# Retention attention and a rational feed-forward: another order of the rounds ahead of the feed-forward

## The chip, the cores and the metric

The kernel runs on one core of one Trainium2 chip. The metric is the device time of one execution in microseconds. Before the change three runs took 1000.58 to 1001.1 us, with a median of 1001.1 us. A separate profiled execution, from which all rows below come, took 999.55 us; the profile's own span, from the first to the last instruction, is 997.8 us of it.

## The reference

Eight batches of 576 tokens with eight heads of 64 go through causal attention with a decay instead of a softmax, and the result, as one matrix of 4608 x 512, through a feed-forward whose activation is a quotient of two polynomials:

```
scores = (1/8) * q @ k.T                       # per batch and head
Dmat[i, j] = gamma[h] ** (i - j) if i >= j else 0
x = ((scores * Dmat) @ v) as 4608 x 512
h = x @ w_in                                   # 512 x 2048
P = a0 + a1*h + a2*h^2 + a3*h^3
Q = 1 + |b0|*|h| + |b1|*h^2
out = (P / (Q + 1e-6)) @ w_out                 # 2048 x 512
```

All data are float32.

## The kernel before

**Attention, in units.** The 4608 tokens are 36 units of 128. For unit n the kernel loads a transposed pair q, k (the tile `qk`) and an untransposed pair k, v (the tile `kv`), 512 KB each (`load_unit`). Then, in this order of need:

- `scale_q(n)` multiplies q by a table of decays: one pass on GpSimd (POOL).
- `scale_v(n)` multiplies v by a decay per head: eight small passes on ScalarE (ACT).
- `scores(n)` forms k times q on TensorE (PE) into a PSUM tile `ps`; `decay(n)` masks it on VectorE (DVE) into `s`.
- `outputs(n)` adds three products on PE into the same `ps`: s with v, k with v (the state's increment, called `ds`), and the running state `S_sb` with q.
- `keep_hi(n)` copies the result to `xhi` on ACT, rounded to the type that the fast matmul takes; `keep_lo(n)` writes what the rounding lost to `xlo` on DVE, and then, on DVE too, adds `ds` to the state `S_sb` (or copies it, for the first unit of a batch).
- `fade(n)` multiplies `S_sb` by a decay on POOL. The next unit's `outputs` needs the faded state.

**Feed-forward, in steps.** There are nine blocks of 512 tokens (four units each) and sixteen slices of the hidden width; a step is one slice of one block. `gemm1` makes a slice h from `xhi` and `xlo`, the `ffn_...` parts compute the activation on ACT, DVE and (for one pass in the first 24 steps) POOL, and `gemm2` adds its product to the block's output, three to four steps later. So that both matmuls are accurate, each of the 32 weight tiles is split once into a rounded and a remaining part: `start` takes the magnitude of the bits on ACT (`c`), `split0` is one pass of DVE on `c`, `split1` and `split2` are one pass each of DVE with the bits as second operand, and `split3` makes the rounded part on ACT (`w`) and the rest on POOL (`w`). The names with a number, such as `c0_3`, `w0_3`, `bits0_3`, mean w_in's tile 3; with 1 in front, w_out's.

**What sets the order.** Each engine executes its instructions in the order in which they are written. A table of names gives this order: `BEFORE` for the rounds ahead of the feed-forward (round n = 0 to 4 handles a new unit n and the outputs of unit n-1), `FIRST` for the first 24 steps, `DENSE` for the next 8, `REST` for all others. `run` walks through the table and calls what is due. `STARTS_BEFORE` and `STARTS` say how many weights are started in each round and each step. Units 4 to 8 are handled inside `FIRST`; units 0 to 3, the first block, must be complete, `xhi` and `xlo`, before the first `gemm1`. All loads are issued by SyncE (SP) in the order in which they are written: units 0 to 5 and eight weights up front, the rest as the steps go; a load also waits until an earlier one has completed, and for its buffer.

Two rules of the framework matter for the change. A PSUM bank of a tile has one reader or writer at a time in the written order, so of two instructions of different engines that read the same `ps`, the second waits for the first. And the score tiles of units 2 and 4 share one PSUM buffer, so `scores(4)` waits until unit 2's `keep_lo` is done.

Of the kernel before, what the change touches and what calls it, by code (L numbers as in the profile page):

```python
# [12 lines left out]
F32 = mybir.dt.float32  # L13
# [17 lines left out]
NP = 4  # L31

BEFORE = "scale_q split1 scale_v split2 split3 start scores outputs decay split0 keep_hi keep_lo fade".split()
FIRST = (
    "split1 gemm1 outputs ffn_p split2 ffn_hi keep_hi ffn_lo gemm2 ffn_r scale_q split3 keep_lo fade start ffn_p2"
    " scale_v scores decay split0 ffn_q ffn_v"
).split()
DENSE = (
    "gemm1 outputs keep_hi split1 keep_lo fade ffn_p split2 split0 ffn_v scale_q ffn_hi ffn_r ffn_lo scale_v gemm2"
    " ffn_p2 scores decay split3 ffn_q"  # L40
).split()
REST = (
    "gemm1 ffn_p outputs keep_hi keep_lo fade ffn_hi ffn_p2 ffn_lo scores decay scale_q scale_v ffn_v gemm2 ffn_r ffn_q"
).split()
END = "ffn_r ffn_hi gemm2 ffn_lo ffn_q".split()

STARTS_BEFORE = [0, 1, 1, 1, 2]
STARTS = [1, 2, 2, 1, 2] + [1] * 19

# [17 lines left out]
def retention_ffn(ctx: ExitStack, tc: tile.TileContext, qkv, w_in, w_out, ab, masks, gq, gv, out):  # L67
# [185 lines left out]
    def keep_lo(n):  # L253

        u = n % 9
        o, ds = parts_of(n)
        hi, lo = (x_part(x, n) for x in x_of(n // 4))
        dve.tensor_tensor(lo, o, hi.bitcast(F32), ALU.subtract)
        if u in (0, 4):
            dve.tensor_copy(S_sb, ds)  # L260
        elif u != 8:
            dve.tensor_tensor(S_sb, S_sb, ds, ALU.add)
        del st_a[n]

# [174 lines left out]
    nc.sync.dma_start(ab_sb, ab)
    for n in range(NP + 1):  # L440
        before(n)
# [10 lines left out]
    for i in range(len(steps) + lag(len(steps))):  # L452
# [63 lines left out]
```

## Time and profile before

| what | us |
|---|---|
| median of three runs | 1001.1 |
| the profiled execution | 999.55 |
| its span | 997.8 |
| first `gemm1` matmul begins | 44.15 |
| PE busy in the span | 934.3 |
| DVE busy in the span | 839.0 |
| ACT busy in the span | 709.0 |
| POOL busy in the span | 158.3 |
| DMA queue for all loads and stores, share of 16 engines | 17.9% |

The rows of the timeline give start, length, engine, operation, the tile written and the tiles read, a count, and in brackets how long the engine was idle before and what ended it. Buffer numbers are left out there, so `ps` stands for each unit's tile. `PEld` is the weight load that goes ahead of a matmul. A line number L63 is that of a helper through which all engine instructions pass, so groups are told apart by tile names. The granted clock of TensorE has a mean of 0.978.

### The profile page before, as it was taken

Reading aid. Unit: us, or ns where it says so; the run is one execution under the profiler, and the core shown is the slowest. Engines: PE = TensorE matmul, PEld = TensorE weight load, DVE = VectorE, ACT = ScalarE, POOL = GpSimd, SP = SyncE. Lnnn points to the kernel's source line nnn. Section 1 sums busy time; section 2 is a strip of 40 time slices with the busy share of each in tenths; the row PEclk is TensorE's granted clock in tenths of the full one; section 3 lists DMA queues with packets and bytes.
Section 4 is the critical chain, followed back from the end, with each engine's and each line's share of the span. In section 5 each row is a group of like instructions: output and inputs, shape, how many; then the busy total and the mean of one; then the engine's idle time right before and its main releaser. Section 6 shows DMA issues by size and latency. Waiting matters only on the chain.

```text
span 997.8 us, 14766 instructions
## 1 busy us (share of the span) xinstructions
PE 934.3 (94%) x5658; PEld 756.3 (76%) x5658; DVE 839.0 (84%) x1189; ACT 709.0 (71%) x1274; POOL 158.3 (16%) x128
## 2 busy tenths in 40 slices
PE   5687878788999999999999999999999999999998
PEld 5566766566787888878888888888878888888886
DVE  3499989999788888888888888988888888888895
ACT  4386777777767777777777777777777777777774
POOL 2444433443100000100000000100000000000000
PEclk8798999999999999999999999999999999999999
DMA  9943100002212111210121112111211121001001
GB/s 359 407 178 127 43 0 1 1 0 82 89 43 85 44 43 43 85 64 22 43 85 43 43 44 85 43 43 43 85 43 43 43 85 44 1 1 43 1 1 42
DMA packets 20550, 65.31 MB, mean 65 GB/s; under 512 B 2304, under 2 KB 2432, under 8 KB 20480
## 3 DMA queue, kind: packets, MB, share of 16 engines
q1 hardware_dynamic: 20480, 64.37, 17.9%
q8 instruction: 44, 0.72, 0.3%
q14 instruction: 26, 0.21, 0.1%
HBM read 54.93 MB, written 9.44 MB: 65 GB/s over the span
## 4 chain that ended last, share of the span: by engine, by line
PE 73%; DVE 16%; ACT 5%; issue 3%; DMA 2%; POOL 0%; SPq 0%; ACTq 0%; POOLq 0%
PE acc L63 33%; PE h L63 31%; PE ps L63 9%; DVE c L63 7%; DVE p L63 6%; DVE v L63 2%; DMA qk<-in_qkv 2%; ACT c L63 1%; ACT u L63 1%; ACT kv L63 1%; ACT o L63 1%; ACT v L63 1%; DMA kv<-in_qkv 1%; ACT g L63 0%; POOL qk L63 0%
## 5 line engine op out<-in xcount | busy, mean ns | idle before, releaser
L63 PE MATMUL acc<-w,g 128*128 128x512 f32 x1632 | 404.9, 397 | 5.2 <-ACT o L63 4.0
L63 PE MATMUL h<-xhi,w 128*128 128x512 f32 x1152 | 381.1, 392 | 17.9 <-DVE p L63 17.2
L63 PEld LDWEIGHTS acc<-w,g 128*128 128x128 f32 x1632 | 305.2, 190 | 77.4 <-ACT o L63 4.8
L63 PEld LDWEIGHTS h<-xhi,w 128*128 128x128 f32 x1152 | 216.5, 188 | 69.4 <-DVE p L63 22.7
L63 PE MATMUL h<-xlo,w 128*128 128x512 f32 x576 | 224.6, 390 | 0.2 <-DVE xlo L63 0.2
L63 ACT ACTIVATE p<-h,ab_sb 128x512 f32<-128x512 f32 x144 | 111.4, 773 | 135.2 <-PE h L63 135.1
L63 DVE TENSOR_TENSOR v<-v,u 128x512 f32<-128x512 f32 x144 | 124.4, 864 | 27.9 <-ACT v L63 27.9
L63 DVE SCALAR_TENSOR_TENSOR p<-p,ab_sb,u 128x512 f32<-128x512 f32 x144 | 108.8, 756 | 27.2 <-ACT u L63 26.4
L63 ACT ACTIVATE u<-h 128x512 f32<-128x512 f32 x144 | 85.7, 595 | 61.8 <-DVE v L63 60.4
L63 DVE TENSOR_TENSOR p<-p,h 128x512 f32<-128x512 f32 x144 | 98.9, 687 | 33.9 <-ACT u L63 33.2
L63 PEld LDWEIGHTS h<-xlo,w 128*128 128x128 f32 x576 | 108.3, 188 | 22.4 <-DVE xlo L63 0.5
L63 ACT ACTIVATE v<-u,absb 128x512 f32<-128x512 f32 x144 | 116.2, 807 | 1.3 <-DVE p L63 1.1
L63 POOL TENSOR_TENSOR S_sb<-S_sb,gv_sb 128x256 f32<-128x256 f32 x32 | 21.8, 680 | 583.3 <-DVE S_sb L63 583.3
L63 DVE SCALAR_TENSOR_TENSOR p<-p,ab_sb,h 128x512 f32<-128x512 f32 x144 | 107.2, 744 | 3.1
L63 ACT ACTIVATE u<-u,lnb 128x512 f32<-128x512 f32 x144 | 104.4, 725 | 4.7
L63 DVE SCALAR_TENSOR_TENSOR p<-v,p 128x512 f32<-128x512 f32 x144 | 101.6, 706 | 5.0
L63 ACT ACTIVATE u<-v,lnb 128x512 f32<-128x512 f32 x144 | 103.1, 716 | 0.1
L63 DVE SCALAR_TENSOR_TENSOR v<-v,u 128x512 f32<-128x512 f32 x144 | 99.4, 690 | 0.0
L63 ACT ACTIVATE g<-p 128x512 fp32r<-128x512 f32 x136 | 85.7, 630 | 8.0 <-DVE p L63 4.3
L63 DVE TENSOR_TENSOR g<-p,g 128x512 fp32r<-128x512 f32 x112 | 77.6, 693 | 1.4 <-ACT g L63 1.4
L63 ACT ACTIVATE kv<-kv,gv_sb 128x64 f32<-128x64 f32 x288 | 72.5, 340 | 6.2 <-DMA gv_sb<-in_gv 5.0
L63 POOL TENSOR_TENSOR qk<-qk,gq_sb 128x512 f32<-128x512 f32 x36 | 59.7, 1660 | 9.5 <-DMA qk<-in_qkv 9.5
(35 smaller groups left out, 634.6 us busy)
## 6 DMA issues: line engine op xcount, KB each, us to landing
qk<-in_qkv SPq DMA_DIRECT2D x36, 512.0 KB, 4.8
kv<-in_qkv SPq DMA_DIRECT2D x36, 512.0 KB, 3.9
bits<-in_w_in SPq DMA_DIRECT2D x16, 512.0 KB, 10.2
bits<-in_w_out SPq DMA_DIRECT2D x16, 512.0 KB, 10.2
out<-o SPq DMA_DIRECT2D x16, 512.0 KB, 3.2
out<-o SPq DMA_DIRECT2D x4, 256.0 KB, 2.3
gq_sb<-in_gq SPq DMA_DIRECT2D x1, 256.0 KB, 2.7
mask_sb<-in_masks SPq DMA_DIRECT2D x1, 128.0 KB, 4.5
```

The lines of the kernel that those rows point to most:

```text
L63: return lambda *a, **k: self.tc.keep_in_program_order(method(*a, **k))
```

## The change

In the rounds ahead of the feed-forward, `scale_q` and `scale_v` are called for unit n+1 instead of unit n, with unit 0 scaled ahead of round 0. In the table they stand at the front of the round, ahead of the fade. The state's addition, until now the second half of `keep_lo`, is a function `add` of its own. In all four tables it stands ahead of `keep_lo`; in `BEFORE` it and the fade stand ahead of `keep_hi` as well. The splits' places in `BEFORE` are others too, and of the weights one is started in round 3 instead of step 1.

```diff
-BEFORE = "scale_q split1 scale_v split2 split3 start scores outputs decay split0 keep_hi keep_lo fade".split()
+BEFORE = "split1 start scale_q scale_v scores decay outputs split2 add fade keep_hi keep_lo split3 split0".split()
 FIRST = (
-    "split1 gemm1 outputs ffn_p split2 ffn_hi keep_hi ffn_lo gemm2 ffn_r scale_q split3 keep_lo fade start ffn_p2"
+    "split1 gemm1 outputs ffn_p split2 ffn_hi keep_hi ffn_lo gemm2 ffn_r scale_q split3 add fade keep_lo start ffn_p2"
     " scale_v scores decay split0 ffn_q ffn_v"
 ).split()
...
-STARTS_BEFORE = [0, 1, 1, 1, 2]
-STARTS = [1, 2, 2, 1, 2] + [1] * 19
+STARTS_BEFORE = [0, 1, 1, 2, 2]
+STARTS = [1, 1, 2, 1, 2] + [1] * 19
...
     def keep_lo(n):
 
+        hi, lo = (x_part(x, n) for x in x_of(n // 4))
+        dve.tensor_tensor(lo, parts_of(n)[0], hi.bitcast(F32), ALU.subtract)
+        del st_a[n]
+
+    def add(n):
+
         u = n % 9
-        o, ds = parts_of(n)
-        hi, lo = (x_part(x, n) for x in x_of(n // 4))
-        dve.tensor_tensor(lo, o, hi.bitcast(F32), ALU.subtract)
+        ds = parts_of(n)[1]
         if u in (0, 4):
             dve.tensor_copy(S_sb, ds)
         elif u != 8:
             dve.tensor_tensor(S_sb, S_sb, ds, ALU.add)
-        del st_a[n]
...
-        todo |= {f.__name__: (f, n) for f in (decay, scale_q, scale_v)}
+        todo["decay"] = decay, n
+        if n < NP:
+            todo |= {f.__name__: (f, n + 1) for f in (scale_q, scale_v)}
         if n >= 1:
-            todo |= {f.__name__: (f, n - 1) for f in (keep_hi, keep_lo, fade)}
+            todo |= {f.__name__: (f, n - 1) for f in (keep_hi, add, keep_lo, fade)}
             todo["outputs"] = (put_out, n - 1)
...
     nc.sync.dma_start(ab_sb, ab)
+    scale_q(0)
+    scale_v(0)
     for n in range(NP + 1):
         before(n)
```

`DENSE` and `REST` change as `FIRST` does (`keep_lo fade` becomes `add fade keep_lo`), and the steps' list of due calls takes `add` in.

**POOL, rounds 2 and 3.** Before, from the fade of unit 1's state on; `qk3` and `qk4` are the queries of units 3 and 4, `w0_1` the remaining part of a weight:

```order
L63 TENSOR_TENSOR S_sb_111<-S_sb_111,gv_sb_93 128x256
L63 TENSOR_TENSOR qk3_131<-qk3_131,gq_sb_94 128x512
L63 TENSOR_TENSOR w0_1_293<-c0_1_240,w0_1_293 128x512
L63 TENSOR_TENSOR S_sb_111<-S_sb_111,gv_sb_93 128x256
L63 TENSOR_TENSOR qk4_139<-qk4_139,gq_sb_94 128x512
```

POOL in the changed kernel, from the queries of unit 3 on; the first fade in it is that of unit 1's state again:

```order
L63 TENSOR_TENSOR qk3_131<-qk3_131,gq_sb_94 128x512
L63 TENSOR_TENSOR S_sb_111<-S_sb_111,gv_sb_93 128x256
L63 TENSOR_TENSOR w0_0_287<-c0_0_188,w0_0_287 128x512
L63 TENSOR_TENSOR qk4_139<-qk4_139,gq_sb_94 128x512
L63 TENSOR_TENSOR S_sb_111<-S_sb_111,gv_sb_93 128x256
```

The queries have moved from behind the fade to in front of it, and the weight's pass stands right behind the fade and belongs to a weight one earlier.

**ACT, rounds 2 to 4.** Before, from `keep_hi(1)` (into `xhi0` from `ps1`) to `keep_hi(3)`:

```order
L63 ACTIVATE xhi0_220<-ps1_190 128x4x128
L63 ACTIVATE kv3_133<-kv3_133,gv_sb_93 128x64 x8
L63 ACTIVATE w0_1_293<-c0_1_240 128x512
L63 ACTIVATE c0_2_296<-bits0_2_135 128x512
L63 ACTIVATE xhi0_220<-ps2_242 128x4x128
L63 ACTIVATE kv4_141<-kv4_141,gv_sb_93 128x64 x8
L63 ACTIVATE w0_2_349<-c0_2_296 128x512
L63 ACTIVATE c0_3_352<-bits0_3_137 128x512
L63 ACTIVATE c1_0_354<-bits1_0_143 128x512
L63 ACTIVATE xhi0_220<-ps3_298 128x4x128
```

ACT in the changed kernel, from the values of unit 3 to the same `keep_hi(3)`:

```order
L63 ACTIVATE kv3_133<-kv3_133,gv_sb_93 128x64 x8
L63 ACTIVATE xhi0_230<-ps1_199 128x4x128
L63 ACTIVATE w0_0_287<-c0_0_188 128x512
L63 ACTIVATE c0_2_292<-bits0_2_135 128x512
L63 ACTIVATE c0_3_294<-bits0_3_137 128x512
L63 ACTIVATE kv4_141<-kv4_141,gv_sb_93 128x64 x8
L63 ACTIVATE xhi0_230<-ps2_247 128x4x128
L63 ACTIVATE w0_1_345<-c0_1_236 128x512
L63 ACTIVATE c1_0_352<-bits1_0_143 128x512
L63 ACTIVATE c0_4_354<-bits0_4_145 128x512
L63 ACTIVATE xhi0_230<-ps3_305 128x4x128
```

Each unit's values now stand ahead of the `keep_hi` of the unit two before it, and the second of the two weights started in round 3 is `c0_3`.

**DVE, rounds 2 and 3.** Before, from `keep_lo(1)` (into `xlo0` from `ps1`) on; `s3` is `decay(3)`:

```order
L63 TENSOR_TENSOR xlo0_221<-ps1_190,xhi0_220 128x4x128
L63 TENSOR_TENSOR S_sb_111<-S_sb_111,ps1_190 128x256
L63 SCALAR_TENSOR_TENSOR c0_1_240<-bits0_1_129,c0_1_240 128x512 x2
L63 TENSOR_TENSOR s3_331<-ps3_298,mask_sb_92 128x1024
L63 TENSOR_SCALAR c0_2_296<-c0_2_296 128x512
L63 TENSOR_TENSOR xlo0_221<-ps2_242,xhi0_220 128x4x128
L63 TENSOR_TENSOR S_sb_111<-S_sb_111,ps2_242 128x256
```

DVE in the changed kernel, from the same `keep_lo(1)` to the two passes of `split0` that follow `keep_lo(2)`:

```order
L63 TENSOR_TENSOR xlo0_231<-ps1_199,xhi0_230 128x4x128
L63 TENSOR_SCALAR c0_1_236<-c0_1_236 128x512
L63 SCALAR_TENSOR_TENSOR c0_1_236<-bits0_1_129,c0_1_236 128x512
L63 TENSOR_TENSOR s3_314<-ps3_305,mask_sb_92 128x1024
L63 SCALAR_TENSOR_TENSOR c0_1_236<-bits0_1_129,c0_1_236 128x512
L63 TENSOR_TENSOR S_sb_111<-S_sb_111,ps2_247 128x256
L63 TENSOR_TENSOR xlo0_231<-ps2_247,xhi0_230 128x4x128
L63 TENSOR_SCALAR c0_2_292<-c0_2_292 128x512
L63 TENSOR_SCALAR c0_3_294<-c0_3_294 128x512
```

The addition to the state has moved ahead of `keep_lo`, and between the two stand three passes on one weight and the mask, where there were the mask and passes on two weights.

**DVE, steps 1 and 2.** Before, from `decay(5)` on; `p`, `v`, `u` are the activation's tiles of steps 0 to 2:

```order
L63 TENSOR_TENSOR s5_520<-ps5_511,mask_sb_92 128x1024
L63 TENSOR_SCALAR c1_1_506<-c1_1_506 128x512
L63 TENSOR_SCALAR c0_5_508<-c0_5_508 128x512
L63 SCALAR_TENSOR_TENSOR p0_0_443<-p0_0_443,ab_sb_95,u0_0_441 128x512
L63 SCALAR_TENSOR_TENSOR v0_0_442<-v0_0_442,u0_0_441 128x512
L63 SCALAR_TENSOR_TENSOR p0_0_443<-v0_0_442,p0_0_443 128x512
L63 TENSOR_TENSOR v0_1_495<-v0_1_495,u0_1_494 128x512
L63 SCALAR_TENSOR_TENSOR c1_1_506<-bits1_1_151,c1_1_506 128x512
L63 SCALAR_TENSOR_TENSOR c0_5_508<-bits0_5_153,c0_5_508 128x512
L63 TENSOR_TENSOR p0_2_578<-p0_2_578,h0_2_535 128x512
L63 SCALAR_TENSOR_TENSOR c1_1_506<-bits1_1_151,c1_1_506 128x512
L63 SCALAR_TENSOR_TENSOR c0_5_508<-bits0_5_153,c0_5_508 128x512
```

DVE in the changed kernel, the same stretch:

```order
L63 TENSOR_TENSOR s5_526<-ps5_517,mask_sb_92 128x1024
L63 TENSOR_SCALAR c0_5_514<-c0_5_514 128x512
L63 SCALAR_TENSOR_TENSOR p0_0_451<-p0_0_451,ab_sb_95,u0_0_449 128x512
L63 SCALAR_TENSOR_TENSOR v0_0_450<-v0_0_450,u0_0_449 128x512
L63 SCALAR_TENSOR_TENSOR p0_0_451<-v0_0_450,p0_0_451 128x512
L63 TENSOR_TENSOR v0_1_503<-v0_1_503,u0_1_502 128x512
L63 SCALAR_TENSOR_TENSOR c0_5_514<-bits0_5_153,c0_5_514 128x512
L63 TENSOR_TENSOR p0_2_582<-p0_2_582,h0_2_539 128x512
L63 SCALAR_TENSOR_TENSOR c0_5_514<-bits0_5_153,c0_5_514 128x512
```

The three passes on one of the two weights are gone from here. They stand in the rounds now.

More of the change, by code (lines that the diff above doesn't have):

```diff
@@ L38 @@
 DENSE = (
-    "gemm1 outputs keep_hi split1 keep_lo fade ffn_p split2 split0 ffn_v scale_q ffn_hi ffn_r ffn_lo scale_v gemm2"
+    "gemm1 outputs keep_hi split1 add fade keep_lo ffn_p split2 split0 ffn_v scale_q ffn_hi ffn_r ffn_lo scale_v gemm2"
     " ffn_p2 scores decay split3 ffn_q"
@@ L42 @@
 REST = (
-    "gemm1 ffn_p outputs keep_hi keep_lo fade ffn_hi ffn_p2 ffn_lo scores decay scale_q scale_v ffn_v gemm2 ffn_r ffn_q"
+    "gemm1 ffn_p outputs keep_hi add fade keep_lo ffn_hi ffn_p2 ffn_lo scores decay scale_q scale_v ffn_v gemm2 ffn_r ffn_q"
 ).split()
 END = "ffn_r ffn_hi gemm2 ffn_lo ffn_q".split()
-STARTS_BEFORE = [0, 1, 1, 1, 2]
-STARTS = [1, 2, 2, 1, 2] + [1] * 19
+STARTS_BEFORE = [0, 1, 1, 2, 2]
+STARTS = [1, 1, 2, 1, 2] + [1] * 19
 SCORES = [1, 3, 5, 23, 25, 27, 29, *range(2 * NF, (NB - 1) * NF, 4)]
@@ L458, in retention_ffn @@
             out_n = due.pop()
-            todo |= {f.__name__: (f, out_n) for f in (keep_hi, keep_lo, fade)}
+            todo |= {f.__name__: (f, out_n) for f in (keep_hi, add, keep_lo, fade)}
             todo["outputs"] = (put_out, out_n)
```

## The prediction

> **What bounds the kernel now.** I read the table of stretches first. Its rows give, for a stretch of the span, its length, the busy time of PE, PEld, DVE, ACT and POOL with their instruction counts, then TensorE's granted clock, the DMA share and GB/s.
>
> ```profile
> 20.00:40.00 20.00, 10.96 (x132) 9.74 (x132) 8.35 (x13) 7.92 (x23) 7.67 (x6) 0.67 1.03 407
> 60.00:80.00 20.00, 13.14 (x96) 10.41 (x94) 19.93 (x26) 14.84 (x29) 10.53 (x8) 0.84 0.08 30
> 112.00:232.00 120.00, 97.08 (x434) 74.50 (x433) 109.48 (x148) 87.84 (x142) 49.39 (x35) 0.98 0.01 1
> 300.00:400.00 100.00, 99.42 (x602) 80.59 (x602) 87.76 (x124) 71.14 (x130) 9.26 (x8) 1.00 0.16 53
> ```
>
> There are three stages. In the rounds no engine is busy for more than 55% (10.96 of 20 us): a loop of waits sets the pace. From the first step to about 232 us DVE does (19.93 of 20, later 109.48 of 120). After that PE does (99.42 of 100). The stages follow each other, and neither of the later two waits for anything that comes by the clock, so what the rounds lose or gain is carried to the end whole. Next, the chain that ended last, in the rounds (start, length, what):
>
> ```profile
> 7.09 9.54 DMA qk<-in_qkv
> ...
> 16.64 9.47 DMA qk<-in_qkv
> ...
> 35.20 0.04 POOL S_sb L63
> 35.24 0.85 issue
> 36.09 1.72 POOL qk L63
> ...
> 37.85 5.62 PE ps L63 x64
> ...
> 43.50 0.61 ACT xhi L63
> ...
> 44.13 0.70 DVE xlo L63
> ```
>
> The loop is fade, scaling of the next queries, scores and outputs, `keep_hi`, `keep_lo`, addition, fade. The timeline of one turn (fade of unit 1 to addition of unit 2):
>
> ```profile
> 24.69 0.41 DVE L63 TENSOR_TENSOR S_sb<-S_sb,ps 128x256 f32<-128x256 f32 x1
> 25.24 0.93 POOL L63 TENSOR_TENSOR S_sb<-S_sb,gv_sb 128x256 f32<-128x256 f32 x1 [5.97 <-DVE S_sb L63]
> 26.13 1.71 POOL L63 TENSOR_TENSOR qk<-qk,gq_sb 128x512 f32<-128x512 f32 x1
> 27.80 1.27 POOL L63 TENSOR_TENSOR w<-c,w 128x512 fp32r<-128x512 f32 x1
> 27.90 2.08 PE L63 MATMUL ps<-qk 64*128 64x128 f32 x16 [4.51 <-POOL qk L63]
> 30.02 1.23 DVE L63 TENSOR_TENSOR s<-ps,mask_sb 128x1024 f32<-128x1024 f32 x1 [3.31 <-PE ps L63]
> 33.41 0.60 ACT L63 ACTIVATE xhi<-ps 128x512 fp32r<-128x512 f32 x1 [5.42 <-PE ps L63]
> 33.90 2.01 ACT L63 ACTIVATE kv<-kv,gv_sb 128x64 f32<-128x64 f32 x8
> 34.04 0.69 DVE L63 TENSOR_TENSOR xlo<-ps,xhi 128x512 fp32r<-128x512 f32 x1 [2.45 <-ACT xhi L63]
> 34.65 0.41 DVE L63 TENSOR_TENSOR S_sb<-S_sb,ps 128x256 f32<-128x256 f32 x1
> ```
>
> One turn is 34.65 - 24.69 = 9.96 us, and POOL, PE, ACT and DVE take it in turn. The queries of unit 3, issued at 7.09, landed at 16.63 but are scaled at 26.13, only because POOL's order puts them behind the fade. (The chain also names a transfer that ends at 26.12, issued at 16.64. That is unit 5's, and I take it for a coincidence; it is a rival below.)
>
> **The change: the rounds.** With the queries and values scaled a round sooner the loop is cut. What is late next is the data. In ACT's new order the values of unit n+1 stand ahead of `keep_hi(n-1)`, so a load holds a `keep_hi`. SP's rows (start and length of the issue), then the loads' times to landing in the same order:
>
> ```profile
> 7.62 0.51 SPq L104 DMA_DIRECT2D kv<-in_qkv  x1
> 12.82 0.33 SPq L104 DMA_DIRECT2D kv<-in_qkv  x1
> 22.93 0.33 SPq L439 DMA_DIRECT2D ab_sb<-in_ab  x1
> ```
>
> ```profile
> kv<-in_qkv SPq DMA_DIRECT2D x1, 512.0 KB, 11.5
> kv<-in_qkv SPq DMA_DIRECT2D x1, 512.0 KB, 11.4
> ab_sb<-in_ab SPq DMA_DIRECT2D x1, 3.0 KB, 9.1
> ```
>
> Unit 3's values land at 19.1, unit 4's at 24.2, the activation's constants at 32.0. SP's order up to there is unchanged, so these times hold. The passes on a weight, in the view of tile `c` (shortest, median, longest, in ns):
>
> ```profile
> L63 DVE SCALAR_TENSOR_TENSOR c<-bits,c x62: 677/686/1785, 15.2 to 226.4; 128x512 int32<-128x512 int32 x62
> L63 ACT ACTIVATE c<-bits x32: 644/652/680, 12.2 to 228.1; 128x512 f32<-128x512 f32 x32
> L63 DVE TENSOR_SCALAR c<-c x32: 415/1068/1514, 12.9 to 229.3; 128x512 int32<-128x512 int32 x32
> ```
>
> Now the new path. Values of unit 3 at 19.1, scaled in 2.01 (21.1); `keep_hi(1)` 0.60 (21.7); `keep_lo(1)` 0.69 (22.4). DVE then has a split pass 0.42, another 0.69, the mask 1.23 and a third pass 0.69: 3.03 (25.4). A POOL pass on a weight lies beside them; for that I add 0.7 (26.1, why see below). Addition 0.41 (26.5), `keep_hi(2)` behind it 0.60 and `keep_lo(2)` 0.69 (27.8). Unit 4's scaled values (24.2 + 2.0 = 26.2) are just in time, so that load is hidden, with 0.3 us to spare. `scores(4)` needs unit 2's buffer and so this `keep_lo`; with `outputs(3)` PE takes 5.5 us, as the piece of 5.62 in the chain shows (33.3). Addition 0.41, `keep_hi(3)` 0.60, and six hand-overs of some 0.03 us: `keep_lo(3)` begins at **34.5 instead of 44.13, 9.6 us sooner**.
>
> The ends of this term. PE is idle for some 5 us before `scores(4)`, and after such an idle time scores take 2.08 us; in the first round they took less:
>
> ```profile
> 6.81 1.16 PE L63 MATMUL ps<-qk 64*128 64x128 f32 x16 [1.98 <-POOL qk L63]
> ```
>
> By that ratio PE would need 3.1 us instead of 5.5, but then DVE is late: two first split passes, two second ones, mask and two third ones are 2 x 0.42 + 4 x 0.64 + 1.23 = 4.6 us. So the term reaches 9.6 + 0.9, and without the 0.7 beside POOL 11.2. Downwards, two full POOL passes (1.27 each) on DVE's line instead of 0.7, and as much behind `scores(4)`, take off some 2.2: 7.4.
>
> **The change: beside POOL.** Two rows of one place in step 2, and DVE's passes on the two weights started in step 1:
>
> ```profile
> 68.56 1.28 POOL L63 TENSOR_TENSOR w<-c,w 128x512 fp32r<-128x512 f32 x1
> 68.66 1.46 DVE L63 TENSOR_SCALAR c<-c 128x512 int32<-128x512 int32 x1
> 59.02 0.92 DVE L63 TENSOR_SCALAR c<-c 128x512 int32<-128x512 int32 x2
> 62.46 2.39 DVE L63 SCALAR_TENSOR_TENSOR c<-bits,c 128x512 int32<-128x512 int32 x2
> 65.36 1.79 DVE L63 SCALAR_TENSOR_TENSOR c<-bits,c 128x512 int32<-128x512 int32 x2
> ```
>
> A pass of 0.42 us that meets a POOL pass takes 1.46 and ends 0.28 us after it: DVE stood until POOL was done. So each POOL pass put beside DVE's split passes costs between 0 and 1.27, and I take about half, 0.7. One such place is in the path above. The other is step 0: there four split passes of DVE used to lie beside the fade and the queries; now POOL also has two weight passes of 1.27 there (`w0_2`, `w0_3`), which were at other times before. I take **0.7 lost** in step 0, between 0 and 1.3.
>
> The Trainium skill, "SBUF — State Buffer", section "Who interferes with whom", states this as a rule: VectorE and GpSimd share one pair of ports as an exclusive lock, held for the whole instruction, by VectorE when it has two SBUF inputs or runs in a two-port mode. By that rule and the trace this change pays for the cover it takes; with the durations of undisturbed passes alone, the sum below would be 12.9 instead of 11.5.
>
> **The change: one weight less in the steps.** In steps 1 and 2 the three passes on one of two weights go: half of 0.92, 2.39 and 1.79 is **2.6 us** on DVE, the engine that sets the pace there. At least 0.42 + 2 x 0.60 = 1.6 goes (0.60 is DVE's step from one 0.68 us pass to the next). At most, if the pass that met POOL is the one that goes, it is 0.4 + 1.7 + 0.7, and 1.0 in the pass at 68.66, whose POOL neighbour leaves too: 3.8. The cost comes back in round 3 and 4, counted above.
>
> **At nothing.** The swap of addition and `keep_lo` in the steps: both stand side by side as before, `keep_lo` ends 0.41 later, and who waits is a `gemm1` two steps on.
>
> ```profile
> L63 PE MATMUL h<-xlo,w 128*128 128x512 f32 x576 | 224.6, 390 | 0.2 <-DVE xlo L63 0.2
> ```
>
> PE waited 0.2 us for all `xlo` together, so nothing is near; without that slack it would be 0.41 for each unit. In SP's queue the load of unit 8's queries moves ahead of two weights' bits and waits for `outputs(6)`, now some 70 us; the later of these weights is started near 215 (the last ACT pass on `c` is at 228.1). The constants at 32.0 are wanted when h is there, 34.5 + 3.4.
>
> **Sum.** 9.6 - 0.7 + 2.6 = 11.5 us. Against the profiled execution's 999.55 (span 997.8 and 1.75 around it) that is 988.05; the median of the runs is 1.55 higher, 1001.1, so I forecast **989.6**. With all ends at once: 7.4 - 1.3 + 1.6 = 7.7 (993.4) to 11.2 + 3.8 = 15.0 (986.1).
>
> **Rivals.**
> 1. The late transfer. If the queries of unit 3 really come at 26.12, as the chain can be read, the fade behind them ends at 26.13 + 1.71 + 0.93 = 28.8, `outputs(2)` at 29.5, `keep_lo(2)` at 31.2 and `keep_lo(3)` begins at 37.9: 6.2 sooner, in all 8.1, **993.0**. Against it stands that SP issued the load at 16.64 as soon as the one of 7.09 had landed, and that POOL sat 5.97 us idle for DVE, not for a load, just before.
> 2. No stalls beside POOL, or fewer: 12.9 to 15.0 gained, **987.2** or so. For it: the times of meeting are a matter of tenths.
> 3. Slower. DVE's split pass and POOL's weight pass meet in each of the 21 steps from 3 to 23. The median first pass is 1.07 against the shortest 0.42, so on average half a POOL pass is paid already; if the shift puts them in full meeting, another 0.6 a step is 12.6 us, and the kernel ends at 989.6 + 12.6, **1002.2**. It decides from 11.5 / 21 = 0.55 a step. Against it: from step 3 on no engine's order changes but for the swap, so the steps should fall into the same pattern.
> 4. The change doesn't do what it says: the start is sooner, but the steps then wait for something at a fixed time, such as weights, and end as before, **1000** to 1002. Against it: DMA's share is 0.08 from 60 us on.
>
> **Chances.** The forecast (9.4 to 12.9 gained) 0.73; rival 2 0.12; rival 1 0.06; 7.7 to 9.4 for other reasons 0.03; rivals 3 and 4 0.03 each. A measurement tells about 0.2% (2 us) from no change. Faster 0.94, same 0.03, slower 0.03. The range takes the ends of the terms, 986.1 to 993.4.
>
> **What would show it.** `keep_lo(3)` near 34.5 and the first `gemm1` just before it; POOL's scalings of units 2 to 4 close to their loads; `scores(4)` right behind `keep_lo(2)` near 27.8. The pass below is the first of step 3's activation; it should begin 11.5 sooner, near 64.2, and the end as much.
>
> ```profile
> 75.67 0.68 DVE L63 TENSOR_TENSOR p<-p,h 128x512 f32<-128x512 f32 x1
> ```
>
> I am wrong if `keep_lo(3)` comes after 37 (the rounds' term), if the step from there to this pass is not 1.9 us shorter than 31.5 (the weight and the stalls), or if the distance from this pass to the end grows (rival 3 or 4).

## The result, and the profile after

The changed kernel takes **988.29 us** (median of 987.77 to 988.92), against 1001.1 before (1000.58 to 1003.93): 12.8 us less, a ratio of 0.9863 with a 95% interval of 0.985 to 0.9877. The forecast was 989.6. The profiled execution took 987.99 us with a span of 986.2, which is 11.6 below the span of before.

The same stretches as in the prediction, in the changed kernel (busy time of PE, PEld, DVE, ACT and POOL with counts, granted clock, DMA share, GB/s):

```profile
20.00:40.00 20.00, 10.89 (x130) 9.05 (x129) 17.44 (x22) 9.51 (x25) 8.16 (x8) 0.79 1.03 406
60.00:80.00 20.00, 14.54 (x103) 11.76 (x103) 19.93 (x27) 15.88 (x35) 11.43 (x10) 0.83 0.19 64
112.00:232.00 120.00, 98.51 (x453) 76.00 (x453) 110.26 (x150) 89.36 (x148) 48.73 (x34) 0.99 0.03 9
300.00:400.00 100.00, 99.43 (x633) 80.81 (x632) 85.82 (x125) 71.49 (x131) 8.80 (x9) 1.00 0.15 53
```

In the first row DVE went from 8.35 to 17.44 us busy. The stretch holds 2.9 us of step 0 in the changed kernel; from `keep_lo(0)` to `keep_lo(3)` alone DVE is busy for 16.62 of 19.21 us, and before it was for 12.82 of 29.85. The loop of waits is gone, and DVE is nearly full, in part with standing beside POOL. The other rows are those of before: DVE sets the pace to about 230 us, PE afterwards.

The timeline of the changed kernel over the rounds, with the path to the end of the first block (start, length, engine, what, and the idle time before with what ended it):

```profile
17.93 1.28 POOL L63 TENSOR_TENSOR qk<-qk,gq_sb 128x512 f32<-128x512 f32 x1 [0.49 <-DMA qk<-in_qkv]
...
19.16 2.02 ACT L63 ACTIVATE kv<-kv,gv_sb 128x64 f32<-128x64 f32 x8 [0.75 <-DMA kv<-in_qkv]
...
21.87 0.41 DVE L63 TENSOR_TENSOR S_sb<-S_sb,ps 128x256 f32<-128x256 f32 x1
22.32 0.60 ACT L63 ACTIVATE xhi<-ps 128x512 fp32r<-128x512 f32 x1 [1.13 <-DVE S_sb L63]
...
22.95 0.69 DVE L63 TENSOR_TENSOR xlo<-ps,xhi 128x512 fp32r<-128x512 f32 x1 [0.67 <-ACT xhi L63]
...
23.51 1.28 POOL L63 TENSOR_TENSOR w<-c,w 128x512 fp32r<-128x512 f32 x1 [0.53 <-ACT w L63]
23.55 1.51 DVE L63 TENSOR_SCALAR c<-c 128x512 int32<-128x512 int32 x1
...
24.74 1.45 POOL L63 TENSOR_TENSOR qk<-qk,gq_sb 128x512 f32<-128x512 f32 x1
25.10 1.63 DVE L63 SCALAR_TENSOR_TENSOR c<-bits,c 128x512 int32<-128x512 int32 x1
...
28.39 0.41 DVE L63 TENSOR_TENSOR S_sb<-S_sb,ps 128x256 f32<-128x256 f32 x1
28.84 0.60 ACT L63 ACTIVATE xhi<-ps 128x512 fp32r<-128x512 f32 x1 [1.70 <-DVE S_sb L63]
...
29.46 0.69 DVE L63 TENSOR_TENSOR xlo<-ps,xhi 128x512 fp32r<-128x512 f32 x1 [0.66 <-ACT xhi L63]
...
30.41 2.08 PE L63 MATMUL ps<-qk 64*128 64x128 f32 x16 [6.72 <-DVE xlo L63]
...
37.07 0.69 DVE L63 TENSOR_TENSOR xlo<-ps,xhi 128x512 fp32r<-128x512 f32 x1 [0.66 <-ACT xhi L63]
```

The reader is to see four things. POOL scales unit 3's queries when their load lands (17.93), not behind a fade. ACT is idle ahead of both `keep_hi`, and what ends that is the addition (`<-DVE S_sb`), not the load. Two DVE passes take 1.51 and 1.63 where undisturbed ones take 0.42 and 0.69; each ends only after the POOL pass beside it has ended (24.79 and 26.19). And the last `xlo`, `keep_lo(3)`, begins at 37.07; forecast was 34.5, before it was 44.13.

### The profile page after: what moved, and what is told of

It reads as the page before. It is cut to its first block, busy times and chain, and to the rows that moved or that the text cites. A ratio compares the mean times of both kernels' runs of the same rounds, so it can differ in the third digit from the quotient of the medians.

```text
span 986.2 us, 14758 instructions
## 1 busy us (share of the span) xinstructions
PE 929.7 (94%) x5658; PEld 752.2 (76%) x5658; DVE 829.3 (84%) x1189; ACT 708.0 (72%) x1274; POOL 146.1 (15%) x128
## 4 chain that ended last, share of the span: by engine, by line
PE 71%; DVE 19%; ACT 5%; issue 3%; DMA 1%; SPq 0%; ACTq 0%; DVEq 0%
PE acc L63 32%; PE h L63 31%; PE ps L63 8%; DVE c L63 8%; DVE p L63 7%; DVE v L63 2%; ACT c L63 1%; ACT u L63 1%; DMA kv<-in_qkv 1%; ACT kv L63 1%; ACT v L63 1%; DVE s L63 1%; ACT o L63 1%; DMA qk<-in_qkv 0%; DVE xlo L63 0%
## 5 line engine op out<-in xcount | busy, mean ns | idle before, releaser
L63 DVE TENSOR_TENSOR v<-v,u 128x512 f32<-128x512 f32 x144 | 99.5, 691 | 27.8 <-ACT v L63 27.7
L63 DVE TENSOR_TENSOR g<-p,g 128x512 fp32r<-128x512 f32 x112 | 90.2, 805 | 1.4 <-ACT g L63 1.4
L63 DVE SCALAR_TENSOR_TENSOR c<-bits,c 128x512 int32<-128x512 int32 x64 | 57.8, 914 | 0.1
```

What stands on the lines that cost most here:

```text
L63: return lambda *a, **k: self.tc.keep_in_program_order(method(*a, **k))
```

## The experiments

Six marks serve as a ruler: the starts of `keep_lo(0)` and `keep_lo(3)`, and the first DVE pass of the activation (`p<-p,h`) in steps 0, 3, 24 and 34. "Span" is that of the profiled execution, all from its start, in us.

| kernel | lo(0) | lo(3) | step 0 | step 3 | step 24 | step 34 | span |
|---|---|---|---|---|---|---|---|
| before | 14.28 | 44.13 | 49.00 | 75.67 | 234.58 | 306.33 | 997.8 |
| before_again | 16.18 | 46.31 | 51.18 | 77.84 | 236.71 | 308.47 | 999.9 |
| changed | 17.86 | 37.07 | 43.52 | 67.29 | 226.24 | 295.41 | 986.2 |
| after_again | 17.86 | 36.72 | 43.17 | 66.94 | 225.84 | 297.59 | 988.2 |
| scale_as_before | 17.60 | 44.60 | 51.07 | 74.83 | 233.79 | 302.95 | 993.7 |
| values_late | 16.61 | 35.54 | 41.33 | 65.09 | 224.00 | 295.77 | 986.6 |
| old_starts | 17.66 | 37.25 | 42.12 | 68.79 | 227.76 | 299.53 | 990.3 |
| old_tables | 17.33 | 36.07 | 42.52 | 66.32 | 225.24 | 297.02 | 988.2 |
| add_late | 17.29 | 33.60 | 39.00 | 63.27 | 222.12 | 292.26 | 983.3 |
| split0_early | 16.45 | 34.62 | 40.95 | 64.72 | 223.61 | 295.35 | 986.1 |
| warm | 16.78 | 35.38 | 41.16 | 64.94 | 223.88 | 294.06 | 984.8 |
| late_warm | 16.94 | 34.32 | 39.72 | 64.00 | 222.84 | 292.96 | 983.9 |
| late_split0_warm | 16.68 | 32.87 | 37.73 | 62.16 | 221.01 | 293.67 | 984.8 |
| fewer_warm | 17.59 | 32.80 | 37.67 | 62.11 | 220.96 | 291.13 | 982.1 |

### Both kernels once more: before_again, after_again

No edit.

> The kernel before once more, for its profile. If the two stretches of low TensorE clock that the first trace shows between 230 and 260 us (the products at 231.4 took 4.28 us, those at 254.1 took 4.62, against 3.02 and 3.01 in the changed kernel) belong to that one execution, they are absent or elsewhere here, and the distance from step 24's first activation pass to step 34's is up to 2.9 us shorter than 71.75. If they belong to the kernel's order, both rows are low again and the distance is 71.75 within 0.3.

> The changed kernel once more, with five rounds. If the first profile stands for it: keep_lo(3) begins at 37.1 and step 3's first activation pass at 67.3, both within 0.5, the time 988.3 within 1, a gain of 12 to 13.5. If the 0.5 to 1 us by which its first loads came late was chance, both come up to 1 us sooner.

Measured: 1001.65 us in one run for the first, and for the second 989.07 (987.8 to 990.2), ratio 0.9874 (0.9859 to 0.9889). The table shows what repeats and what does not. From `keep_lo(3)` to step 0, and from there to step 3, both pairs agree within 0.01 us. Two stretches do not repeat. The start of the rounds lies at 14.28 in one execution of before and at 16.18 in the other. TensorE's clock goes with it: between 10 and 14 us the granted clock is 1.00 in the first and 0.50 in the second, and unit 1's scores take 1.16 and 2.08 us (first and second execution):

```profile
10.31 1.16 PE L63 MATMUL ps<-qk 64*128 64x128 f32 x16 [1.47 <-POOL qk L63]
```

```profile
10.31 2.08 PE L63 MATMUL ps<-qk 64*128 64x128 f32 x16 [0.44 <-POOL qk L63]
```

In the first execution of the changed kernel the clock of these 4 us is 0.50 too, and unit 1's scores take 2.08 us in both of its executions, so the first pair sets a quick start against a slow one. And from step 24 to step 34 three executions took 71.75 or 71.76 us while the first one of the changed kernel took 69.17. That is TensorE's clock as well. In the first execution of before (the group of twelve products into `acc`, on PE):

```profile
231.37 4.28 PE L63 MATMUL acc<-w,g 128*128 128x512 f32 x12
...
246.54 3.02 PE L63 MATMUL acc<-w,g 128*128 128x512 f32 x12
...
254.08 4.62 PE L63 MATMUL acc<-w,g 128*128 128x512 f32 x12 [1.80 <-ACT o L63]
```

The same place in the first and in the second execution of the changed kernel:

```profile
244.75 3.01 PE L63 MATMUL acc<-w,g 128*128 128x512 f32 x12 [1.79 <-ACT o L63]
```

```profile
245.35 4.61 PE L63 MATMUL acc<-w,g 128*128 128x512 f32 x12 [1.80 <-ACT o L63]
```

One program, the same idle time ahead of it, and one time 3.01, the other 4.61 us. The table of stretches gives clock 0.83 for 240 to 250 us in the second execution, and 1.00 in the first. The other profiles below fall on both sides: of all 14, this group takes 3.0 to 3.1 us in six (changed, scale_as_before, add_late, warm, late_warm, fewer_warm) and 4.6 in eight. So 2.6 us of the first profile's 11.6 is luck of that execution, and spans of single profiles can't be compared to better than that; the second pair, with the slow groups in both, differs by 11.7 all the same, since there the rounds gained more, both executions having run those scores slowly.

### Scaling not sooner: scale_as_before

```diff
-            todo |= {f.__name__: (f, n + 1) for f in (scale_q, scale_v)}
+        todo |= {f.__name__: (f, n) for f in (decay, scale_q, scale_v)}
```

(and the two calls ahead of round 0 go)

> The changed kernel, but each unit's queries and values are scaled in their own round, as before; addition and fade stay ahead of keep_hi. If the scaling a round sooner is what cuts the loop (the record's main step): the loop is back, a turn takes 9 to 10 us, keep_lo(3) begins at 41 to 44 instead of 36.1 to 37.1, and the time is 994 to 998. If the addition ahead of keep_hi and keep_lo does a good part of it: a turn takes at most 8.7 (9.96 less keep_hi and keep_lo, 1.3), keep_lo(3) begins below 41 and the time is below 994.

Measured: 996.09 us (992.78 to 997.56), ratio 0.9946 (0.9927 to 0.9964). `keep_lo(3)` begins at 44.60, between nothing sooner and 1.7 sooner than in the two profiles of before. From `keep_lo(0)` on it takes 27.00 us, against 29.85 and 30.13 before and 18.86 to 19.21 in the changed kernel. The loop is back: POOL scales unit 4's queries at 36.44, behind the fade (34.07) again, and behind a weight's pass.

```profile
33.57 0.42 DVE L63 TENSOR_TENSOR S_sb<-S_sb,ps 128x256 f32<-128x256 f32 x1 [1.41 <-PE ps L63]
34.07 0.61 POOL L63 TENSOR_TENSOR S_sb<-S_sb,gv_sb 128x256 f32<-128x256 f32 x1 [5.92 <-DVE S_sb L63]
...
35.22 1.27 POOL L63 TENSOR_TENSOR w<-c,w 128x512 fp32r<-128x512 f32 x1 [0.53 <-ACT w L63]
...
36.44 1.45 POOL L63 TENSOR_TENSOR qk<-qk,gq_sb 128x512 f32<-128x512 f32 x1
...
37.94 2.08 PE L63 MATMUL ps<-qk 64*128 64x128 f32 x16 [4.51 <-POOL qk L63]
...
44.60 0.69 DVE L63 TENSOR_TENSOR xlo<-ps,xhi 128x512 fp32r<-128x512 f32 x1 [0.66 <-ACT xhi L63]
```

So the scaling a round sooner is worth 7.0 to 7.8 us of the change and cuts the loop. That the addition's place does nothing for the loop, this run does not show. The addition begins 0.13 us after the outputs here (33.44), and 1.32 after them before (33.33 to 34.65, with `keep_hi` and `keep_lo` between). But the weight's pass, which stood behind the queries before, stands ahead of them now: from the addition to the next scores it takes 4.37 us, and before 3.21 (24.69 to 27.90). The two cancel, and a turn takes 9.94 us as against 9.96. Without the weight's pass in it a turn would be some 8.8 us, an estimate from these rows; no run has that order.

Of the 4.9 us that the rest still gains, steps 0 to 3 are 2.9 and the way from `keep_lo(3)` to step 0 takes back 1.6. The other 3.6 belongs to no step that I can name: the runs themselves lie 4.8 apart, and this profile, like the first of the changed kernel, had the quick groups after step 24.

### Only the queries sooner: values_late

```diff
-            todo |= {f.__name__: (f, n + 1) for f in (scale_q, scale_v)}
+            todo["scale_q"] = scale_q, n + 1
+        todo["scale_v"] = scale_v, n
```

> Of the changed kernel, only the queries are scaled a round sooner; the values' pass on ScalarE stands in its own round again. Theory 1: the loop was cut by the queries alone, since the scores wait for GpSimd's pass over them and nothing of the loop waits for the values' pass: keep_lo(3) at 36 to 37.5, the time within 0.5 of the changed kernel's 988 to 989. Theory 2: both count, since the values' pass (2.0) stands ahead of the keeping's first half on ScalarE: one to three rounds longer by up to 2.0, the time 990 to 994.

Measured: 988.54 us (984.01 to 988.76), ratio 0.9863 (0.984 to 0.9887): the changed kernel's time. `keep_lo(3)` comes 18.93 us after `keep_lo(0)`, against 19.21 and 18.86 in the changed kernel. Unit 4's values pass now runs beside the wait for PE and holds nothing:

```profile
28.56 0.69 DVE L63 TENSOR_TENSOR xlo<-ps,xhi 128x512 fp32r<-128x512 f32 x1 [0.66 <-ACT xhi L63]
...
29.51 2.08 PE L63 MATMUL ps<-qk 64*128 64x128 f32 x16 [6.72 <-DVE xlo L63]
...
31.02 2.00 ACT L63 ACTIVATE kv<-kv,gv_sb 128x64 f32<-128x64 f32 x8
```

The queries alone carry the gain; the values sooner are worth nothing measurable.

### The weight back in step 1: old_starts

```diff
-STARTS_BEFORE = [0, 1, 1, 2, 2]
-STARTS = [1, 1, 2, 1, 2] + [1] * 19
+STARTS_BEFORE = [0, 1, 1, 1, 2]
+STARTS = [1, 2, 2, 1, 2] + [1] * 19
```

> The changed kernel with the weights started as before (one in round 3, two in step 1). Theory by the recorded terms: round 3 and 4 lose two split passes each and their meetings with POOL, so keep_lo(3) begins 0.5 to 2 us sooner than 37.1, but step 3's first activation pass comes 1 to 2.5 later than 67.3, and the time is 1 to 2.5 above the changed kernel's. Rival: the weight costs in the rounds what it saves in the steps; then step 3's pass and the time stay within 0.5.

Measured: 990.02 us (988.71 to 992.26), ratio 0.9886 (0.9869 to 0.9902), beside 0.9874 for the changed kernel on the same chip. From `keep_lo(3)` to step 3 it takes 31.54 us, to the hundredth what before takes, where the changed kernel takes 30.22. The weight one round earlier is thus worth 1.32 us between these two profiles: 2.9 gained in steps 0 to 3, 1.58 lost ahead of step 0. But step 0's products ran at full clock here and slowly in the changed kernel, so the 1.58 is not the weight's alone. Where they ran at full clock with the weight in the rounds (values_late, warm) it takes 29.55 and 29.56 us from `keep_lo(3)` to step 3, and the weight is worth 2.0. The difference of the medians, 0.95, is inside the two intervals. `keep_lo(3)` itself is no sooner without the weight (19.59 from `keep_lo(0)`), but DVE then waits 2.10 us for PE, which ran at half clock there:

```profile
36.17 0.42 DVE L63 TENSOR_TENSOR S_sb<-S_sb,ps 128x256 f32<-128x256 f32 x1 [2.10 <-PE ps L63]
```

So the rounds carry the extra weight for nothing as long as TensorE is slow in them; what it would cost there at full clock was not run.

### The steps' tables as before: old_tables

```diff
-    "split1 gemm1 outputs ffn_p split2 ffn_hi keep_hi ffn_lo gemm2 ffn_r scale_q split3 add fade keep_lo start ffn_p2"
+    "split1 gemm1 outputs ffn_p split2 ffn_hi keep_hi ffn_lo gemm2 ffn_r scale_q split3 keep_lo add fade start ffn_p2"
```

(and the same swap in `DENSE` and `REST`; here and in `add_late`, `late_warm`, `late_split0_warm` and `fewer_warm` the line `del st_a[n]` goes from `keep_lo` too, since the addition behind it still needs the entry)

> The changed kernel, but in the steps' three tables the addition stands behind keep_lo as before. Theory: the swap is not free of effect. In the steps from 24 on the fade and the scaling of the next queries on POOL start 0.6 us sooner by it, and DVE's product of v and u no longer waits for them: here that product takes 1.58 us again in the steps with outputs, instead of 0.92 to 0.98, and the shift against before gained between steps 24 and 34 is 0.7 to 2 us smaller; the time is 0.7 to 2 above the changed kernel's. Rival (the whole 2.6 us gained between steps 24 and 34 is TensorE's clock): the time is the changed kernel's within 0.4, whatever the product takes. Up to step 23 both expect no change within 0.2.

Measured: 988.54 us (987.19 to 990.14), ratio 0.9864 (0.9848 to 0.9881). The theory is right about the rows and wrong about their price. DVE's product of v and u takes 1.40 to 1.78 us again in the steps with outputs from step 24 on, where the changed kernel has at most 0.99, but from step 24 to step 34 it is 71.78 us, as in after_again (71.75). The whole 2.6 there was the clock. From step 34 to the end old_tables takes 691.2 us, before 691.4, the changed kernel 690.6 to 690.8: about half a microsecond may be the swap's, though late_split0_warm, which has the swap, takes 691.2 too. In the run times no difference shows, which was the price given to the swap.

### The addition behind the keeping in the rounds: add_late

```diff
-BEFORE = "split1 start scale_q scale_v scores decay outputs split2 add fade keep_hi keep_lo split3 split0".split()
+BEFORE = "split1 start scale_q scale_v scores decay outputs split2 keep_hi keep_lo add fade split3 split0".split()
```

> The changed kernel, but in the rounds the addition and the fade stand behind keep_lo. If the addition is needed early (the next outputs wait for the fade): keep_lo(3) begins about 1 us later than 36.1 to 37.1 and the time is 1 above the changed kernel's. Theory now: with the scaling a round sooner the fade is off the path, and DVE's line of split passes is on it; keep_hi(2) then need not wait for the addition (1.70 us of wait in the profile after), keep_lo(2) begins about 1 us sooner and keep_lo(3) 1 to 1.6 sooner; the time is 0.5 to 1.6 below.

Measured: 986.77 us (985.2 to 987.89), ratio 0.9866 (0.9844 to 0.9887), the whole range a little below the changed kernel's 987.8 to 990.2 on that chip, but for one run. From `keep_lo(0)` to `keep_lo(3)` it takes 16.31 us, against 18.86 to 19.21: **2.6 to 2.9 us sooner**. In the last round ACT is released by PE and no longer by DVE:

```profile
22.24 0.42 DVE L63 TENSOR_SCALAR c<-c 128x512 int32<-128x512 int32 x1
...
22.70 0.98 DVE L63 SCALAR_TENSOR_TENSOR c<-bits,c 128x512 int32<-128x512 int32 x1
...
28.06 1.16 PE L63 MATMUL ps<-qk 64*128 64x128 f32 x16 [3.97 <-DVE S_sb L63]
...
32.97 0.60 ACT L63 ACTIVATE xhi<-ps 128x512 fp32r<-128x512 f32 x1 [2.23 <-PE ps L63]
...
33.60 0.69 DVE L63 TENSOR_TENSOR xlo<-ps,xhi 128x512 fp32r<-128x512 f32 x1
```

So of the changed kernel's two halves, the addition's place in the rounds works against it: `keep_hi` may not read `ps` until the addition has, and the addition stands in DVE's queue behind the passes on weights. How much of the 2.6 to 2.9 is that wait is not shown, for two other things changed with it. The two passes that took 1.51 and 1.63 in the changed kernel take 0.42 and 0.98 here (first two rows), as POOL's fade of 0.67 and no longer its longer passes begins beside them. And in the last round the scores began at full clock (1.16 instead of 2.08); the three turns are 1.06, 1.05 and 0.4 to 0.8 us shorter, so the clock can have a part in the last alone.

### A weight's first pass ahead of the keeping: split0_early

```diff
-BEFORE = "split1 start scale_q scale_v scores decay outputs split2 add fade keep_hi keep_lo split3 split0".split()
+BEFORE = "split1 start scale_q scale_v scores decay outputs split2 add fade split0 keep_hi keep_lo split3".split()
```

> The changed kernel, but in the rounds the first split pass stands ahead of keep_hi, so that DVE does it in the 0.66 us in which it waits for keep_hi, and not beside POOL's pass on a weight. If DVE's passes are stretched because they meet POOL's (1.51 instead of 0.42 and 1.63 instead of 0.69 in round 3): one of the two meetings goes, keep_lo(3) begins 1 to 1.5 us sooner, the time is 0.8 to 2 below the changed kernel's. Rival (the stretch is due to something else, such as the loads): the passes stay as long wherever they stand, and keep_lo(3) moves by less than 0.5.

Measured: 988.63 us (986.94 to 990.21), ratio 0.988 (0.9862 to 0.9898). The rounds are 0.7 to 1.0 us shorter (18.17 from `keep_lo(0)` to `keep_lo(3)`), and it does not show in the time. One of the two meetings went, as the theory says, for a little less than its price:

```profile
20.33 0.41 DVE L63 TENSOR_SCALAR c<-c 128x512 int32<-128x512 int32 x1
...
22.32 1.27 POOL L63 TENSOR_TENSOR w<-c,w 128x512 fp32r<-128x512 f32 x1 [1.10 <-ACT w L63]
22.37 1.78 DVE L63 SCALAR_TENSOR_TENSOR c<-bits,c 128x512 int32<-128x512 int32 x1
```

The pass that took 1.51 behind the start of POOL's weight pass takes 0.41 where it begins with POOL idle (POOL's fade starts at 20.49); the next pass now meets the weight's pass and takes 1.78. So the stretch goes with the meeting, and the rival is out.

### TensorE kept busy ahead of step 0: warm

```diff
+KEEP = [0, 0, 0, 22, 3]
...
+    def keep_warm(n):
+        if n and not spin:
+            spin.append(ps_h.tile([P, 512], F32, tag="h", name="spin"))
+        for _ in range(n):
+            pe.matmul(spin[0][:, 0:P], zeros, zeros, start=True, stop=True)
...
+        keep_warm(KEEP[n])
```

> The changed kernel, with 22 products of zeros on TensorE at the end of round 3 and 3 at the end of round 4, in its idle time; nothing else. If TensorE's low clock there comes from its idle time (6.72 us idle, then scores and outputs in 5.45 us, and the first gemm1 in 4.4 instead of 2.8): scores(4) take 1.16, outputs(3) about 2.1, keep_lo(3) begins 0.4 to 0.8 sooner (DVE's passes are next late), the first gemm1 takes 2.8, step 0's first activation pass comes 1 to 2 us sooner, and the time is 1 to 2 below the changed kernel's. Rival: the low clock there has another cause; then these rows stay and the time is the same or later.

Measured: 986.7 us (986.26 to 987.74), ratio 0.9863 (0.9845 to 0.9881). This shows what the way to step 0 costs. In the changed kernel the products of step 0 were still slow half-way (first fence); with the small matmuls ahead of them they were not (second fence):

```profile
39.02 1.05 PE L63 MATMUL h<-xhi,w 128*128 128x512 f32 x2
...
42.23 0.78 ACT L63 ACTIVATE p<-h,ab_sb 128x512 f32<-128x512 f32 x1 [4.06 <-PE h L63]
...
43.52 0.69 DVE L63 TENSOR_TENSOR p<-p,h 128x512 f32<-128x512 f32 x1 [0.62 <-ACT u L63]
```

```profile
37.16 0.62 PE L64 MATMUL h<-xhi,w 128*128 128x512 f32 x2
...
38.88 2.36 DVE L64 SCALAR_TENSOR_TENSOR c<-bits,c 128x512 int32<-128x512 int32 x2
38.96 0.78 ACT L64 ACTIVATE p<-h,ab_sb 128x512 f32<-128x512 f32 x1 [2.48 <-PE h L64]
39.64 0.59 ACT L64 ACTIVATE u<-h 128x512 f32<-128x512 f32 x1
...
41.16 0.68 DVE L64 TENSOR_TENSOR p<-p,h 128x512 f32<-128x512 f32 x1
```

Two products take 1.05 in the one and 0.62 in the other. In the changed kernel DVE stood idle 0.62 us for ACT, and ACT waited for PE: the whole 1.58 us between `keep_lo(3)` and step 0 (6.45 against 4.87) is the clock, and no stall of DVE. The granted clock was 0.50 from 39 to 42 us there, and 1.00 in warm from 36.5 to 38.9. With the clock up, the stall appears: `u` is there at 40.23, but DVE is in its two passes, drawn out to 2.36, until 41.2, so the way is 5.78 us, 0.91 more than before. That it was the small matmuls that raised step 0's clock is not shown: values_late and old_starts have none and ran step 0 at full clock too. For the scores the case is better: they took 2.08 us in all six profiles without small matmuls and with 6.2 to 6.7 us of idle time ahead of them, and 1.16 in all four with small matmuls. Of the 1.6 to 2.4 us by which the time is below the changed kernel's, the marks up to step 3 account for 0.9 to 1.3, taken from `keep_lo(0)`.

### Both together: late_warm, late_split0_warm, fewer_warm

`add_late` and `warm` in one; then also `split0` ahead of the keeping (that one pass of DVE; ScalarE's part, which the expectation names, stays in its place); then 14 small matmuls instead of 22.

```diff
-BEFORE = "split1 start scale_q scale_v scores decay outputs split2 add fade keep_hi keep_lo split3 split0".split()
+BEFORE = "split1 start scale_q scale_v scores decay outputs split2 keep_hi keep_lo add fade split3 split0".split()      # late_warm
+BEFORE = "split1 start scale_q scale_v scores decay outputs split2 split0 keep_hi keep_lo add fade split3".split()      # late_split0_warm
+KEEP = [0, 0, 0, 22, 3]      # late_warm, late_split0_warm
+KEEP = [0, 0, 0, 14, 3]      # fewer_warm
```

> The addition behind the keeping in the rounds (as in add_late) and 25 small matmuls ahead of step 0 (as in warm). add_late's step 0 already ran its seven products at full clock (from keep_lo(3) at 33.60 to step 0's subtraction at 39.00, 5.40, against 6.45 in the first profile of the changed kernel). Theory 1: the two gains are largely the same one, TensorE's clock in step 0, on top of add_late's 3.0 us sooner round. Then keep_lo(3) begins at 33 to 34, step 0's subtraction 5.0 to 5.6 later, and the time is 985.5 to 987.0, within 0.7 of add_late's 986.8. Theory 2: they are two gains (2.3 and 2.4 us against the changed kernel's 989.1), and add: 984.0 to 985.0.

> As late_warm, with a weight's first part (the DVE's integer passes and ScalarE's conversion) started ahead of the keeping and no longer behind it. Theory 1: in a round of the changed kernel the DVE waits for the products ahead of the addition, and a part issued ahead fills that wait: keep_lo(3) up to 1 us sooner than in late_warm, 0 to 1.0 us off the time. Theory 2: since the addition no longer stands ahead of the keeping, nothing is left to wait for there, and the part's passes hold up the keeping: keep_lo(3) later by up to 1.8 us (one lengthened integer pass), the time 0 to 1.5 us longer than late_warm's.

> late_split0_warm with 14 instead of 22 small matmuls ahead of scores(4). In late_split0_warm the 22 (44 passes, 5.18 us from 23.54) ended at 28.65, 1.34 us after keep_lo(2) (26.62 + 0.69 = 27.31), and scores(4) waited for them. 14 take 3.3 us and end near 26.9. Theory 1: DVE becomes the bound, for in late_split0_warm it was idle 0.59 us only between scores(4) and keep_lo(3); so the rounds from keep_lo(0) to keep_lo(3) take 15.6 instead of 16.19 us and the time is 983.9 to 985.0, hardly to be told from 984.8. Theory 2: PE is the bound there, and the whole 1.34 is gained: 14.9 us, the time 983 to 984. Theory 3: the short idle time behind the matmuls lets TensorE's clock drop again: scores(4) take 2.08 instead of 1.16, or the products of step 0 run slowly, and the time is 985.5 to 987.

Measured: late_warm 985.34 us (984.58 to 985.78), ratio 0.984 (0.9819 to 0.986). Its marks at steps 0 and 24 are add_late's or later, as the first theory has it, and the reason is in PE's queue: the small matmuls ended at 30.37 and `scores(4)` waited for them, 2.4 us after `keep_lo(2)` was done (27.28 + 0.69).

```profile
25.26 5.18 PE L64 MATMUL spin<-zeros 128*128 128x128 f32 x44
...
30.37 1.16 PE L64 MATMUL ps<-qk 64*128 64x128 f32 x16
```

What the clock gave, the matmuls that kept it took. The time still came out 1.4 below add_late's, which ran on another chip; that is more than the theory allowed.

late_split0_warm: 984.79 us (984.31 to 986.68), ratio 0.9836 (0.9815 to 0.9856). Its `keep_lo(3)` comes 1.45 us sooner than late_warm's, which is the first theory's direction and a little past its size; the times of the two can't be told apart.

fewer_warm: 986.51 us, in two groups, 983.75 and 983.96 at a mean clock of 0.991, and 986.51 to 986.64 at 0.985 to 0.988; ratio 0.9846 (0.9822 to 0.987). The rounds took 15.21 instead of 16.19 us. From `keep_lo(2)` on it is 0.70, near the 0.59 for which DVE had been idle, and DVE's rows then stand without a gap: DVE is the bound there, as the first theory says; the time misses that theory's 983.9 to 985.0. It lies in the third theory's range, but the scores (1.16) and step 0 ran at full clock, so that theory's cause is not it. Its profile has the shortest span of all, 982.1. But its runs lie 2.5 us apart, and the clock of the execution goes with them; the median is no better than late_split0_warm's.

**The best version** is late_split0_warm. Each of its five runs lies below the lowest of the changed kernel's first eight (987.77), and beside values_late, a stand-in for the changed kernel on the same chip, its median is 3.8 us lower, though one of values_late's five runs took 984.01. The intervals of its ratio and of the changed kernel's (0.985 to 0.9877) still touch.

## Why the prediction was right, and where its terms were off

The sum, 11.5 us, was made for the profiled execution, where 11.6 was measured. By stretches, before minus changed:

| stretch | predicted | first pair | second pair |
|---|---|---|---|
| start to `keep_lo(3)` | 9.6 | 7.06 | 9.59 |
| to step 0's first pass on DVE | -0.7 | -1.58 | -1.58 |
| to step 3's | 2.6 | 2.90 | 2.89 |
| to step 24's | 0 | -0.04 | -0.03 |
| to step 34's | 0 | 2.58 | 0.01 |
| to the end | 0 | 0.68 | 0.82 |
| sum | 11.5 | 11.60 | 11.70 |

**The mechanism was right.** The loop through POOL was the bound of the rounds and the sooner scaling cut it (27.00 us from `keep_lo(0)` to `keep_lo(3)` without it, 18.86 to 19.21 with it; scale_as_before); the queries did it, as the loop named (values_late). The end follows the rounds: from step 3 to step 24 nothing is lost.

**The rounds' term was mis-sized, by 2.57 us in the first profile** (37.07 against 34.5), which passes the bound of 37 that the prediction set itself; the gain of 7.06 also passes the term's lower end, 7.4. (The 2.2 that led to it is not worked out: two full POOL passes instead of 0.7 are 2 x 1.27 - 0.7 = 1.8, and how much it puts behind `scores(4)` is not said.) The path started where it was said to: unit 3's values were there at 19.16, forecast 19.1. Then three parts of it. First, "values of unit 3, scaled, `keep_hi(1)`" has the load hold `keep_hi(1)`; the trace has the addition hold it, which was done at 22.28 on DVE behind the mask and a split pass, so `keep_lo(1)` began at 22.95 and not at 21.7: 1.25. Second, the 0.7 for standing beside POOL: two passes met POOL, one its weight and one its queries, and took 1.51 + 1.63 instead of 0.42 + 0.69, so the stretch to `keep_lo(2)` was 6.51 and not 5.4: 1.11. (The rule that the prediction took from the Trainium skill, "SBUF — State Buffer", section "Who interferes with whom", agrees: each of the two passes lasted until POOL's was done, and ended 0.27 and 0.54 us after it.) Third, the rest, 7.61 and not 7.4: 0.21. The second pair gained 9.59 nevertheless since that execution of before began its rounds 2 us later, with slow scores. Taken from `keep_lo(0)`, the loop itself is 10.6 to 11.3 us shorter (29.85 and 30.13 against 19.21 and 18.86), but `keep_lo(0)` comes 1.7 to 3.6 later.

**Step 0's term left out the clock.** It said 0.7 for DVE beside two more POOL passes. The stall is there and costs 0.91 where nothing covers it (warm; 0.92 in values_late), but in the changed kernel it lay under PE's slow products, which cost 1.58.

**One weight less in the steps** was right in cause and near in size: 2.6 forecast, 2.9 measured, and gone with the weight (old_starts). So the step from `keep_lo(3)` to step 3's pass became 1.32 us shorter, and not 1.9, which was a second sign of being wrong; with step 0 at full clock it became 2.0 (values_late, warm).

**The swap at nothing** was right as far as the times can tell (old_tables). **The addition ahead of the keeping in the rounds** was taken as part of the path and never asked about. For `keep_hi(2)` the prediction did count the DVE passes ahead of it; for `keep_hi(1)` it did not, which is the 1.25 above. With the addition behind the keeping the rounds are 2.6 to 2.9 us shorter (add_late), of which a part is due to other meetings with POOL and perhaps the clock.

**The agreement of the sums is partly luck.** In the first profile a deficit of 2.5 in the rounds and 0.9 in step 0 was made good by 0.3 in the steps, 2.6 from the clock between steps 24 and 34, and 0.7 behind that, of which some half may be the swap's (old_tables) and the rest was not followed.

Of the rivals, the late transfer is out (unit 3's queries were scaled at 17.93, not at 26.1), and so is the one of fewer stalls (there were more). The slower one asked for 0.55 us a step from step 3 on and got 0.04 in all 21; and nothing waited at a fixed time.

## What to carry to other kernels

When a loop is cut, go through the instructions on the new path and ask of each what stands ahead of it in its own queue, not only what it waits for: an addition of 0.41 us behind other work held the keeping 1.1 us longer than the load did. An engine put back in work costs time by what it meets (passes of 0.42 and 0.69 took 1.51 and 1.63) and by the clock at which it starts (1.58 us in step 0). And a control has to leave everything else in place: in scale_as_before a weight's pass went into the loop with the scaling and hid what the addition did. A profile and its sum should be compared stretch by stretch and with a second execution of each kernel: two wrong terms had nearly cancelled here.

## What was not expected of the hardware

- TensorE's clock drops in the middle of full work, in some executions of one program and not in others: behind the same 1.8 us of idle time, twelve products took 3.01 or 4.61 us. The run times fall into two groups some 2 us apart, which fits such a drop but was not followed run by run. The changed kernel repeated gave 987.8 and 988.25, and 989.89 and 990.2, all four at a mean clock of 0.985, so there the mean does not tell them apart. Before gave 1000.01 and 1000.38 at a mean clock of 0.980 and 1001.63 to 1002.44 at 0.975 to 0.977. What decides between them is open.
- Ahead of step 0 the same is seen by kernel: products of step 0 ran slowly in the changed kernel, after_again, old_tables, scale_as_before and split0_early, and at full clock from the third on in the other profiles, though the idle time just ahead of them was alike (in old_starts, which ran them at full clock, 1.24 us, as in the changed kernel). With small matmuls in the idle time `scores(4)` took 1.16 instead of 2.08 us; without any they took 1.16 in add_late too, after 3.97 us of idle time.
- The first loads land at other times from kernel to kernel, and at nearly the same in two profiles of one kernel: unit 0's values were scaled from 7.00 and 7.04 in the two profiles of before, from 8.33 and 8.20 in the changed kernel's, and from 7.21 in late_warm's. Why was not tried.
